# A block-sparse attention with a gated FFN on one Trainium2 core: the first pair's V on another queue, mask rows copied in pieces, the closing blocks in halves, and a new order of all instructions

## The chip, the cores and the metric

The kernel runs on one core of one Trainium2 chip. The metric is the device time of one execution in microseconds (us). Engines are named as in the profile: PE (TensorE matmuls), PEld (PE's weight loads, which overlap its matmuls), DVE (VectorE), ACT (ScalarE), POOL (GpSimd), SP (SyncE, which here only starts transfers). ACT, SP and POOL can each start DMA transfers.

## What is computed

The inputs are q, k and v (4 batches, 8 heads, 768 positions, 64 channels, float32), three sampled key blocks for each of 24 query blocks, and the weights of a gated convolutional feed-forward network.

```python
scores = (q @ k.T) / sqrt(64)
mask   = |blk_i - blk_j| <= 1  or first/last block row or column  or sampled
attn   = softmax(where(mask, scores, -1e9))
x      = (attn @ v), heads side by side          # (4, 768, 512)
h      = relu(x @ w_in)                          # (4, 768, 1024)
c      = conv of 3 taps along the sequence, per channel, with conv_w
out    = (h * sigmoid(c)) @ w_out                # (4, 768, 512) float32
```

## The kernel before, in words

**Tiling.** Two heads make a pair; there are 16 pairs P, four for each batch. The scores come transposed: 128 keys on the partitions, 128 queries in the columns. A pair has 6 key chunks and 6 query chunks for each head. The work of attention is cut into 144 units of eight 128x128 blocks: per unit two groups of score matmuls (line 761, "s"), one exponential of 128x1024 on ACT (line 773, "exp"), two groups of P-times-V matmuls (line 798, "av"). s writes one of two PSUM tiles st0 and st1, exp reads it and writes one of six SBUF tiles pt0 to pt5, and av accumulates in one of two PSUM banks, av0 and av1. V has a 65th column of ones, so the sums of the softmax come out of the same matmuls.

**The mask** needs no operation of its own: the operand tile T of a pair ("slot"; there are five) holds q and k transposed in rows 0 to 63 and, in rows 64 to 87, 24 rows that add -8000 to a masked block: columns 12 to 23 of T (chunks of 128) hold a one for a key's block, columns 0 to 11 the -8000 or 0 of the query's block. These rows are worked out once into slot 0 (line 276 "a1", 285 "a3", 306 "a4", 307 "a5", 314 "m_q0", 317 "m_q1", 322 "m_k", 349 "m_h1", 351 "m_r1"; `away` line 292) and copied to slots 1 to 4 (line 355, "m_slot", 24 partitions x 3072 on DVE). m_k copies from `nblk` (line 286), which is made from the identity matrix `ident`; POOL makes that (line 266) from a tile that DVE has set to zero (line 224), and POOL's DMA issues stand behind it in POOL's list.

**Loads.** The first pair's q, k and v come in float32 by the queues of SP and ACT (lines 244 to 262) and are cast on an engine: v by a copy of 128x768 ("v_cp", line 623). All other pairs come by POOL's queue, which casts to bfloat16 on the way; their V is copied into the tile with the column of ones on DVE or ACT (line 638). For P below 6, q and k are transposed on PE ("k_tr" line 469, "q_tr" lines 502 and 525) and copied from PSUM into the slot ("k_cp" line 480, "q_cp" lines 510 and 531); later ones use the DMA's transposing path (line 597). Units 0 to 17 are the first half of the queries of pairs 0 to 3; unit 4 is the first that needs pair 1, unit 9 pair 2, unit 13 pair 3. Units 18 to 35 are the second half.

**The FFN.** A batch's half of x is normalized (lines 707, 709), transposed, multiplied with w_in (line 895, "f1"), passed through relu by ACT or DVE (lines 915, 917), convolved on DVE (lines 953, 961), gated (lines 1000, 1003, 1008; "g2" is line 1008) and multiplied with w_out (line 830, "f2"), in blocks of 128 positions: `out_block` (line 816) accumulates 8 matmuls of 512 columns in one PSUM bank, copies 128x512 to SBUF ("ev", line 836) and writes it out (line 839). Only the very last block (positions 640 to 767 of the last batch) is done in two halves of 256 columns.

**What sets the order.** The program first makes a list of 1787 operations with their engines and buffers (class `Graph`, line 84). `put_down` (line 95) then walks the string `ORDER` (line 20): two characters give the number of an operation, a letter the engine where there is a choice (V is DVE, A is ACT), and further characters the buffers. So every engine's sequence, every choice between ACT and DVE and every buffer is written out by hand in this string. PE also runs 42 matmuls on zeros ("warm" of 256 columns and "fill" of 128, line 230) in the opening.

Of the kernel before, what the change touches and what calls it, by code (L numbers as in the profile page):

```python
# [25 lines left out]
2o34R1r2G04S2I01s1g4T2J4U6C16D6j26k6v1Z06l16z46L06M1l1p1+V6mV1/V6E51m1t4V2U14W1u4X2W24Y2X4Z1v4+6w6A6B6Q16R6F6N0
6G5U16S16V06W6X21w4/312506O06P6H06I6J05VV6T6+16/6KVih11k73074ii703ik01q2HV4ijV001o7547c17dil7e5in1ioipA17h07i
7m1imViF0iH7j0iGiIiq06U7n7o12b1ir2dV2cVisA7r06Y7s6Z7172767717A17B11iz1iA2Z07t27F07G7f7C32w0iBA2iJiN1iO7H4782iQ
797g7K12p12xV47L2rV2yV7k7l7p2qV7M57P07Q7qit02z17u7viP2BV2AV7w1iR7R07U17V7D0810iKiL7W12K12LV02MV7x82iuivV37E7I7J
7N8618733351347a17O7S7bV1832iS8838b07T7X7Z07Y18c7y08d4iT7+7zViM0iUiw1ixiyViV28g18h2Y1842N0858i58p08q8r0898a8u1  # L30
8v8e8f8j8k8w13522+361372OV2PViW8l28z08A8s08tiY8B27/18E18F8xiC08J08K8y80ViX8m8G38CiD8L48R18SiZ8T52VV0iEVj13j3j2
j918W08Xja8Y08n08D8H8/1908I9408M8oVi+8N1j42/V30Vj5911958U8V8Z8+jf096292jgi/j012j69c1j7j88O18P32V1939d9h09i97jh
jb9e49m19njijjV09j5jc9o139V38V523cjdA19r0989909a9s9w1jo0jp9t3jl11jjqA9x9E0jm9F3d13f9y09G2ju0jv3a0532C0542Q13e
9J19f09g3o3p03l3m1jwA9KjnVjJ0jK9k9O09P9l2D19pjL9L4jM2EV9Q5jr09q9ujs9vjN2FV3r3qjOjtVjR1jS3bV2jT9T19U9V1jA1jBjU
jx0jyjCAjzAjZ29/0a02R1a41a59z9B29A19H9I9M9N9R2TVa13a90aa9CjG08Q2j+jVk09ba602SAab2ae1afag4jD1jP9SjEjFVaj0akjH9W
jQj/jIVjk3h03t13i9D9Xa209Y19Za3k53k1al5jWa7a8acar1jXk6asaw0kj1axat3adahaiamaB1aCan1ay0auavazjYaD4k2kv0aG0aHk8
aI5k7k9ao0k3k4kaaO1kbkcaAkkaPaEaFkwaJaT0aKaL2aMaUkl3x3y23A3B2aQ1kxaY1aV29+3u3s4ap3g3aq03jV3kVkykzA2kmaZb103D3C
3Jb2knA3kB0kCkE1kFkDV14kGVkZ0k+a+3b303vVb61b7b84kN0kObe0aR1bfkQ1kRaSaWaXk/kPA5bj1bkkK0bg5kSAbl1l0l1l2kLbo0kW1a/
bpb0b4b5bt1b9buba0bq33M3N33K0aNbhld1kMVbv2kXbB0bCbikH0kYAbD03wVlf3nA3bG1kIbb1lelg3zV4bckT1bmbnbr3P3OkJV6bH3UbI4
3F03Q13Gl52l7kUkVV7l3bL0bMl6bN5kp0kqbsbwbxbQ1bRbS1bV0bWbdkokrkd1bE1bX33R3E0ll3lml8lol9lhlal41by0kAlblcbzlnlilp  # L40
ljc11ksbFbJbKbOc2c60c7c82ktA0bPbTbAkulk3IV3HVkekfkgc30cb0bUbYlt0lubZ0cccg1khA3lqlr3LV0b+2lscd4lvlz1chlAco0cplB
lCci5lwct1cuc4cq3lDA2lxA0cy0czc5lF13V23X3Y1403Zb/3+lGcv13SV13WV13TVlHVlI0lJcD1c9cElKVm10m2m3cacem4m5cA0cF2lO1cf
cI0cJcK4kilPlL0lMcjcklNAlQVm92ma410mbmcm6m7cl1cr1cQ1cRcS5cscwcV0cWcxcBcCcGcHlR0494a0c01ly4f1c+1c/cX13/46471cL
cN0mdd03lSd30d4lU1lVdb1dccOcmcncP42jelTAmelWVmh1mimjmfmkmgm84ed50dd2cM1cTcUcYcZlX0d1lYmllZVdg0dhdi4l+1l/dl1d2dm
d6d7dq0drm0Amp3de0d82dfdn54b4c4nds1mD1djdkdodpdv1dwdD0dEmx0mEmymmdx3mqd9msdtmrdudydz1dF2dI1dJmtmumnmo4o24s4ddG
dHdN0dOdK4mvmzmFdadP54kdS1dTdLmwmGdMd+0d/dQmA4pdA14l043V2mHV344VmBV0dU1e31dRe4e03dVdWdX0dBe52e80e9mV1mWea0mXV08
dYmY0mZe10e2m+Vnh0ninknjed1ee4glEn21e6m/0ei0ejn0n34B4C34qef4ek5n4A4Geq1ere7ebecegehelev04r4y4Des3n1V9np2nqnsnr
# [12 lines left out]
rn1qKrorC0rdr31rv0rwrDrpreArq1rrrEqTqMrx1rs0qZ0rtqNqOruryqVrzqPqQq+r4rR0rSrL1rMrNrOrTrUqWqXqYrPV1r5r6rVAr7A2q/  # L60
r0rWrQr8r1V0r2rF1rGrHrIrJA3rK
# [52 lines left out]
def kernel(  # L114
# [74 lines left out]
    op = gr.op  # L189
# [53 lines left out]
    vf = m_t[0].rearrange("p x y s -> p (x y s)")[:, 0:1536].bitcast(FP32)  # L243
# [4 lines left out]
    def first_k(x, e, prio, after):  # L248
# [11 lines left out]
    ld_v0 = dma("ld_v0", "SP", lambda: vf.rearrange("p (h c) -> p h c", h=2),  # L260
                v[0, 0:2].rearrange("h (p c) d -> p h (c d)", p=128), -18, service=1.6, after=[q1])
    ld_cw = dma("ld_cw", "SP", lambda: cw0, moe_conv_w.rearrange("k (f p) -> (k f) p", p=128), 8, service=0.05, after=[ld_v0])
# [85 lines left out]

    m_h1 = [op("m_h1", {"DVE": 0.25, "ACT": 0.37}, lambda e: dcopy(e, T_t[0][64:88, 6:11:2], T_t[0][64:88, 0:5:2]), T(0), m_q),
# [3 lines left out]
    mask_ready[(0, 1)] = m_h1  # L353
    for s in range(1, NSLOT):
# [48 lines left out]
    first_nq, first_q_sw = [], []  # L403
# [12 lines left out]
    def kq_transposes(P):  # L416
# [99 lines left out]
        def q_half(g, src, ldq, nbuf, pr):  # L516
            mb = Buf(P_mix)

            def fn(e):
                t = mix_t[mb.index].bitcast(BF16)  # L520
                for y in range(3):
                    nc.tensor.transpose(out=t[:, 128 * y:128 * y + 128], in_=src()[:, 128 * y:128 * y + 128], identity=ident)  # L522
            if P == 0:
                pr = T(14)
            tr = op("q_tr", {"PE": 0.168}, fn, pr, ldq + [o_ident], alloc=[mb], uses=[nbuf], after=k_trs[0:1])
            two = []
            for x in range(2):
                def cp(e, x=x):
                    dcopy(e, T_t[slot.index][0:64, 2 * x + g:2 * x + g + 9:4],
                          mix_t[mb.index].bitcast(BF16)[64 * x:64 * x + 64, 0:384].rearrange("p (c s) -> p c s", s=128))  # L530
                two.append(op("q_cp", {"DVE": t_d2(384) + 0.04, "ACT": t_act(384)}, cp, pr + 0.5 + 0.1 * x, [tr],
                              uses=[mb, slot]))
            for hh in range(2):
                qk_ready[(P, hh, g)] = (two + qk_ready[(P, hh, "k")] + mask_ready[(min(s, NSLOT - 1), hh)] +
                                        (m_r if P == 0 else []))
# [80 lines left out]
    def v_pair(P):  # L616
# [24 lines left out]
        in_turn("first" if P < NF else "v", lv)  # L641
# [21 lines left out]
    first_nq[0].after.append(first_q_sw[0])  # L663

# [151 lines left out]
    def out_block(b, t, due, deps, after, tail=False, last=False):  # L816
        gb, ob = gt_buf[b], Buf(P_os)
        halves = ((0, 256), (256, 512)) if last else ((0, 512),)
        outs = []
        for x, (c0, c1) in enumerate(halves):  # L820
# [6 lines left out]
            for a in range(4):  # L827
# [13 lines left out]
                due + 3, [evo], uses=[ob], dma=("hw", 0.65 if not last else 0.4)))  # L841
# [215 lines left out]
```

## Time and profile before

| | |
|---|---|
| median of 3 runs | 208.72 us (208.53 to 209.41) |
| span of the profiled execution, first to last instruction | 206.8 us |
| so around the span | 1.9 us |
| busy share PE, DVE, ACT, POOL | 96%, 90%, 92%, 30% |
| exp on ACT (144) | 140.6 us, 1048 ns each |

The span is the time between the first and the last instruction of one profiled execution. Busy time is a sum over stages; which engine sets the pace differs from stage to stage, and the ends of matmuls are modelled. A row of a timeline gives start, duration, engine, line, operation, output and input; a row of the chain of waits gives start, length and what held up the end there.

### The profile page before, as it was taken

How to read it: one execution, taken by the hardware profiler on the slowest of the kernel's cores; microseconds unless marked ns; L12 is line 12 of the kernel's file. 1: busy time of each engine (PE TensorE's matmuls, PEld its weight loads, DVE VectorE, ACT ScalarE, POOL GpSimd, SP SyncE). 2: the span in 40 equal slices, each digit the busy share in tenths (PEclk: the TensorE clock that was granted, in tenths of full speed). 3: DMA queues.
4: the chain of work that ended last, by engine and by line, in shares of the span. 5: the costliest groups of instructions: out<-in, count | busy, mean ns of one | idle time of the engine just before them, and what ended most of it. 6: DMA issues, size and time to landing. Idle time of an engine off the chain costs nothing.

```text
span 206.8 us, 6250 instructions
## 1 busy us (share of the span) xinstructions
PE 199.3 (96%) x2418; PEld 142.7 (69%) x2418; DVE 186.4 (90%) x576; ACT 190.6 (92%) x252; POOL 61.9 (30%) x113
## 2 busy tenths in 40 slices
PE   7799999999999999999999999999999999999992
PEld 5587878887567766766676767676667667786750
DVE  7999989999999998999789989999999938999970
ACT  6999999999999999999989998999999979997751
POOL 8696735302843233316054153800000000000000
PEclk9999999999999999999999999999999999999998
DMA  6999999998699976999969659999235131010414
GB/s 156 196 196 185 181 165 132 187 113 77 78 127 142 179 102 93 147 139 193 194 96 107 138 77 170 151 144 130 67 115 87 22 120 51 3 51 5 152 53 153
DMA packets 49305, 25.20 MB, mean 122 GB/s; under 512 B 35100, under 2 KB 46332, under 8 KB 49276
## 3 DMA queue, kind: packets, MB, share of 16 engines
q0 software_dynamic: 19728, 11.05, 44.9%
q1 hardware_dynamic: 29260, 13.46, 33.9%
q8 instruction: 19, 0.31, 0.6%
q10 hardware_dynamic: 288, 0.30, 0.4%
q14 instruction: 10, 0.08, 0.1%
HBM read 23.09 MB, written 6.29 MB: 142 GB/s over the span
## 4 chain that ended last, share of the span: by engine, by line
PE 71%; DVE 14%; ACT 11%; issue 2%; ACTq 0%
PE st L761 22%; PE mix L830 18%; PE mix L895 16%; PE av L798 12%; ACT pt L773 8%; DVE t L331 3%; DVE m L953 3%; DVE m L961 2%; DVE gT L1008 1%; ACT t L327 1%; DVE xtok L709 1%; PE st L830 1%; DVE hE L917 1%; PE mix L728 1%; DVE m L1003 1%
## 5 line engine op out<-in xcount | busy, mean ns | idle before, releaser
L773 ACT ACTIVATE pt<-st 128x1024 bf16<-128x1024 f32 x144 | 140.6, 1048 | 2.4 <-PE st L761 1.3
L761 PE MATMUL st<-t 88*128 88x256 bf16 (+2 forms) x600 | 90.0, 267 | 1.6 <-ACT t L327 0.8
L761 PEld LDWEIGHTS <-t 88*128 88x128 bf16 x600 | 48.5, 97 | 21.4 <-issue 1.6
L798 PEld LDWEIGHTS <-pt 128*128 128x128 bf16 x1152 | 52.2, 97 | 11.5 <-ACT pt L773 1.0
L798 PE MATMUL av<-vt,pt 128*128 128x65 bf16 x1152 | 58.4, 193 | 0.0
L895 PE MATMUL mix<-xT,winb 128*128 128x384 bf16 (+2 forms) x288 | 54.3, 308 | 0.3 <-ACT hE L915 0.2
L953 DVE TENSOR_SCALAR m<-hE,cw 128x382 bf16<-128x382 bf16 (+2 forms) x192 | 48.8, 316 | 0.4
L830 PE MATMUL mix<-woutb,gT 128*128 128x512 bf16 x184 | 48.7, 379 | 0.2 <-DVE gT L1008 0.2
L961 DVE TENSOR_TENSOR m<-m 128x764 bf16<-128x764 bf16 (+2 forms) x64 | 33.8, 534 | 0.6
L895 PEld LDWEIGHTS <-winb 128*128 128x128 bf16 x288 | 24.4, 97 | 9.4 <-issue 0.8
L1000 ACT ACTIVATE m<-m 128x764 bf16<-128x764 bf16 (+2 forms) x32 | 26.8, 840 | 1.1 <-DVE m L961 1.0
L407 POOL COPY pace<-pt 1x1 bf16<-1x1 bf16 x24 | 9.6, 402 | 53.3 <-ACT pt L773 53.3
L830 PEld LDWEIGHTS <-gT 128*128 128x128 bf16 x200 | 17.3, 97 | 11.7 <-DVE gT L1008 1.1
L915 ACT ACTIVATE hE<-mix 128x384 bf16<-128x384 f32 (+2 forms) x36 | 17.7, 507 | 1.7 <-PE mix L895 1.6
L917 DVE TENSOR_SCALAR hE<-mix 128x384 bf16<-128x384 f32 x28 | 15.5, 557 | 4.1 <-PE mix L895 3.7
L1008 DVE TENSOR_TENSOR gT<-m,hE 128x764 bf16<-128x764 bf16 (+3 forms) x36 | 18.2, 511 | 0.6
L709 DVE TENSOR_TENSOR xtok<-av,rcp 128x384 bf16<-128x384 f32 (+2 forms) x36 | 18.1, 508 | 0.5
L239 POOL DMA_DIRECT2D nat<-in_q_dram x23 | 17.0, 738 | 2.1 <-issue 1.4
L331 DVE COPY t<-mix 64x384 bf16<-64x384 bf16 (+1 forms) x33 | 13.4, 413 | 0.7 <-PE mix L522 0.2
L327 ACT COPY o2s<-mix 128x512 f32<-128x512 f32 x17 | 9.9, 598 | 2.9 <-PE mix L830 2.7
L1003 DVE TENSOR_SCALAR m<-m 128x764 bf16<-128x764 bf16 (+3 forms) x36 | 12.1, 335 | 0.5 <-ACT m L1000 0.4
L239 POOL DMA_DIRECT2D vn<-in_v_dram x15 | 11.3, 756 | 1.9 <-DVE vt L331 1.4
(75 smaller groups left out, 118.4 us busy)
## 6 DMA issues: line engine op xcount, KB each, us to landing
out_dram<-o2s SPq DMA_DIRECT2D x23, 256.0 KB, 2.9
nat<-in_k_dram POOLq DMA_DIRECT2D x15, 192.0 KB, 4.2
vn<-in_v_dram POOLq DMA_DIRECT2D x15, 192.0 KB, 5.7
nat<-in_q_dram POOLq DMA_DIRECT2D x6, 192.0 KB, 4.9
winb<-in_moe_w_in_dram POOLq DMA_DIRECT2D x2, 512.0 KB, 7.3
woutb<-in_moe_w_out_dram POOLq DMA_DIRECT2D x4, 256.0 KB, 6.7
nat<-in_q_dram POOLq DMA_DIRECT2D x9, 96.0 KB, 5.2
nq<-in_q_dram POOLq DMA_DIRECT2D x6, 96.0 KB, 5.1
```

What stands on the lines that cost most here:

```text
L239: return op(name, {eng: occ}, lambda e: on(e).dma_start(out=dst(), in_=src), prio, deps, dma=(kind, service), **kw)
L331: nc.vector.tensor_copy(out=dst, in_=src)
L709: nm = op("norm", {"DVE": t_dps(128 * C)}, lambda e: nc.vector.tensor_tensor(out=xtok_t[xk.index][:, 0:C].rearrange("p c h d -> p h c d"), ...
L761: nc.tensor.matmul(out=st[:, 128 * x:128 * (x + n_)], lhsT=t[0:88, 12 + 6 * hh + kc, :], rhs=t[0:88, idx:idx + (n_ - 1) * (2 if P < NPE el ...
L773: nc.scalar.activation(out=pt_t[ptb.index][:, c0:c1], in_=st_t[stb.index][:, c0:c1], func=AF.Exp, bias=0.0, scale=0.125)
L798: nc.tensor.matmul(out=o[:, off:off + 65], lhsT=pt_t[ptb.index][:, 128 * x:128 * x + 128], rhs=V_t[vslot_b[P].index][:, hh, kc, 0:65], sta ...
L830: nc.tensor.matmul(out=acc(), lhsT=gT_t[gb.index][:, ffc, 128 * t:128 * t + 128], rhs=woutb[:, ffc, c0:c1], start=(ffc == 0), stop=(ffc == ...
L895: nc.tensor.matmul(out=mix_t[hb.index][:, w1 * y:w1 * y + w1], lhsT=winb[:, fc, 128 * ffc:128 * ffc + 128], rhs=xT_t[xt_buf[n].index][:, f ...
L953: nc.vector.tensor_scalar(out=m_t[cb.index][:, x, y, 0:w], in0=hE_t[heb.index][:, f0 + y, t0 + x:t0 + x + w], scalar1=cw[:, x, f0 + y:f0 + ...
L961: nc.vector.tensor_tensor(out=m[:, a_, :, 0:w], in0=m[:, a_, :, 0:w], in1=m[:, b_, :, 0:w], op=ALU.add)
L1000: th = [op("tanh", {"ACT": t_act(2 * w) + 0.04}, lambda e, cb=cb, w=w: nc.scalar.activation(out=m_t[cb.index][:, 0, :, 0:w], in_=m_t[cb.in ...
L1008: nc.vector.tensor_tensor(out=gT_t[gtb.index][:, f0:f0 + 2, t0:t1], in0=m_t[cb.index][:, 0, :, 0:w], in1=hE_t[heb.index][:, f0:f0 + 2, 1 + ...
```

## The change

It has four parts.

1. **V of pair 0.** `ld_v0` (float32 by SP's queue into a spare tile) and its cast are gone; pair 0 gets V like the others, in bfloat16 by POOL's queue, with the transfer behind pair 1's q. The copy into the tile with ones, which ACT did, is now given to DVE.
2. **Mask rows.** Slot 1's copy of 24x3072 becomes three: the key columns (24x1536, m_sk), the query columns of the first half (24x768, m_sq) and, later, of the second half (24x768, m_sr). Slot 4's copy becomes a transfer by SP (m_sp). Slots 2 and 3 stay.
3. **Closing blocks.** The two blocks before the last one (positions 384 to 639 of the last batch) are also done in two halves of 256 columns each.
4. **`ORDER`** is another string, for 1801 operations.

```diff
-    ld_v0 = dma("ld_v0", "SP", lambda: vf.rearrange("p (h c) -> p h c", h=2),
-                v[0, 0:2].rearrange("h (p c) d -> p h (c d)", p=128), -18, service=1.6, after=[q1])
...
+    def rows_to(s, c0, c1, step):
+        return lambda e: dcopy(e, T_t[s][64:88, c0:c1:step], T_t[0][64:88, c0:c1:step])
...
     for s in range(1, NSLOT):
-        mr = [op("m_slot", {"DVE": 0.95}, lambda e, s=s: dcopy(e, T_t[s][64:88], T_t[0][64:88]),
-                 T(4.5 * s - 2.5), m_h1 + m_r, earliest=7.0 + 2 * s)]
+        mask_g1[s] = []
+        if s == 1:
+            mr = [op("m_sk", {"DVE": 0.53}, rows_to(1, 12, 24, 1), T(2), m_k + m_h1[1:]),
+                  op("m_sq", {"DVE": 0.33}, rows_to(1, 0, 11, 2), T(2), m_q + m_h1[:1])]
+            mask_g1[s] = [op("m_sr", {"DVE": 0.33}, rows_to(1, 1, 12, 2), T(12), m_r)]
+        elif s < NSLOT - 1:
+            mr = [op("m_slot", {"DVE": 0.95}, lambda e, s=s: dcopy(e, T_t[s][64:88], T_t[0][64:88]),
+                     T(4.5 * s - 2.5), m_h1 + m_r, earliest=7.0 + 2 * s)]
+        else:
+            mr = [dma("m_sp", "SP", lambda s=s: T_t[s][64:88].rearrange("j c s -> j (c s)"),
+                      T_t[0][64:88].rearrange("j c s -> j (c s)"), T(4.5 * s - 2.5), m_h1 + m_r, service=0.3)]
...
-        if P == 0:
-            def cp(e):
-                dcopy(e, V_t[vs.index][:, :, :, 0:64], vf.rearrange("p (h c d) -> p h c d", h=2, c=6))
-            v_ready[P] = op("v_cp", {"DVE": 0.5, "ACT": t_act(768)}, cp, due + 1, [ld_v0] + v_one, alloc=[vs], earliest=8.5)
-            in_turn("vs", v_ready[P])
-            return
...
-        halves = ((0, 256), (256, 512)) if last else ((0, 512),)
+        halves = ((0, 256), (256, 512)) if last or (b == B - 1 and t > 2) else ((0, 512),)
```

The string itself says nothing to a reader. Decoded, the lists of the engines begin like this (numbers count the operations of a name; for copies of q and k, cp means from PSUM).

```
ACT before: q0, k0 issues; m_k0; cast q0, k0, k0; m_q0 twice; q_cp (pair 0); m_q1; m_h1; exp 0; exp 1; v_cp (pair 0); exp 2 ...
ACT after:  q0, k0 issues; m_k0; cast q0, k0, k0; k_cp, q_cp, k_cp (pair 0); cast q0; k_cp (pair 0); exp 0; exp 1; exp 2 ...

DVE before: ones, zeros of hE; zeros of warm, of ident; a1; a3; nblk; m_k1; ident24; m_h1; ones; a4; a5; a5; k_cp; ones, ones;
            k_cp; k_cp; ones; k_cp; m_r1; cast q0; m_slot 1; q_cp (all pair 0); k_cp, k_cp, q_cp, q_cp (pair 1); m_slot 2; cw; diag 4;
            q_cp, q_cp (pair 0, second half); v_cp (pair 1); k_cp, q_cp, q_cp, k_cp (pair 2); rcp, norm 0; v_cp (pair 2);
            m_slot 3; k_cp, k_cp, q_cp, q_cp (pair 3); m_slot 4; rcp, norm 1 ...
DVE after:  a1; a3; ones (3); zeros of warm, of ident; nblk; ident24; ones; m_k1; a4; zeros of hE; a5; ones; m_h1; m_q0 twice;
            k_cp (pair 0); a5; m_sk; m_h1; q_cp (pair 0); m_sq; k_cp, k_cp, q_cp, q_cp (pair 1); m_q1; v_cp (pair 0); m_r1; cw;
            q_cp, q_cp (pair 0, second half); m_slot 2; k_cp, k_cp, q_cp, q_cp (pair 2); v_cp (pair 1); m_slot 3; rcp; v_cp (pair 2);
            norm 0; k_cp, k_cp, q_cp, q_cp (pair 3); diag 4, 6; q_cp, q_cp (pair 2, second half); m_sr; rcp, norm 1 ...

POOL before: iota; ident; loads k1, q1, q0 second half, v1, k2, q2, q1 second half, v2, q2 second half, k3, q3, v3, k4 ...
POOL after:  iota; ident; loads k1, q1, v0, q0 second half, v1, k2, q2, v2, k3, q1 second half, q3, q2 second half, v3, k4 ...
```

In both, pair 0's first av stands behind s of some units on PE: before behind those of units 2 and 3, after behind those of units 4 and 5. Later the two strings hold the same units in the same order, with the FFN's parts at places that differ by a few groups of matmuls. Of the relus of batch 0's first half, two that ACT did (the third and the seventh) are DVE's now; of its second half the first went from DVE to ACT. At the end, PE's last matmuls were those of positions 512 to 639 (8 of 512 columns); now they are the second half of positions 384 to 511 (8 of 256 columns), behind 16 of 256 columns for positions 512 to 639.

More of the change, by code (lines that the diff above doesn't have):

```diff
@@ L26 @@
[L26 to L35, printed above, removed]
@@ new lines @@
+ef0egmZA0846Vn0Ve4n11e8eh04f4m4u4r4n14s4D4E34tek1ele9n2edeeem54I4A4F4B24G4Hnj0nkn3V9nld+nmes0etein70ejn41eneu3ex1n5
+n6Aeyeo1evn8ez1eC0eDna1mEdE24ilA4v0ep1eqernr1n9VansnbnnncV4jV34kVnz2eE44OeH1eIng0nheweAeBeFeP0eJ0eGnd1eKniAno4P0eQ
+eR2eLnemL0eU1eVnueM0nAeNnfAbnH3ntnpnvnInCnBeZ0e+mMmNeW54l47d/mK4weO4J14KlGe/3f21f3nK4oV3nDnJ4CV4nq0f41mR1eS0nwnx
+4xV4nynLf70f8mOmPA1eTff1mSmTeXfgf90nEeYmUmVA0f0fk0f1flf5fh4fm2f6fao50o81o9o6fc1oaVfp1o7Afqfb1fin/1fu0fr5nMnF4yVnG
+ov0ownNo20o0o3o1Vo4Aon1fdnOfjfnfofvfsfC1ftfDnV0fw3fE1oyopoxoznWfH0fIfJ0nXnYnZA3fM1fxfNfO4fyob1fR0fSfF0fGoe0oc4LV0
@@ L62 @@
+hE0hP0hhVhz1pCApShAVpYp/3hQhY1hZhFhJqs0qm1qnq0hR3hL0q1hMq2pZq3h+1i10hK1hSi2hTqoAgqtq71ia1ibq8h/0hU1p+qD0q4q5hVq6
+quAhqT1qUqVqWqEi30hN0q9qai0hOA2ic4qj0qki4qbA1i51idieqp1qlAii62i7i80if0qv2qwqxigqGqqi9Aqd0qrAjqehW1qfhXVih1qgiiArq1
+rrqFqyqHqzqhA0rh0rirsAqArjAqL3qNqXqBqCrn1rorpAqIrt0rk0rup8qcpeqirv2qMqJrwqKqOrxqPrlrmArD1q/1rEry0rzqYrA0rF2qQrBqZrG
+rCrHqRr0rZ0rI0s31r50rJr6rK0qSr+r/s4s5r7r1rLrMq+r8r2s0s6r9V3r3A1s1A2rarN0rOrT1rPrQs7ArRA0r4s8s2rSrUrVrWrb0rcrXArYrd
+rerfArg
 """
@@ L259 @@
     ld_q0, ld_k0 = [q0, q1], [k0, k1]
-    ld_v0 = dma("ld_v0", "SP", lambda: vf.rearrange("p (h c) -> p h c", h=2),
-                v[0, 0:2].rearrange("h (p c) d -> p h (c d)", p=128), -18, service=1.6, after=[q1])
-    ld_cw = dma("ld_cw", "SP", lambda: cw0, moe_conv_w.rearrange("k (f p) -> (k f) p", p=128), 8, service=0.05, after=[ld_v0])
+    ld_cw = dma("ld_cw", "SP", lambda: cw0, moe_conv_w.rearrange("k (f p) -> (k f) p", p=128), 8, service=0.05, after=[q1])
     o_iota = op("iota", {"POOL": 0.15}, lambda e: nc.gpsimd.iota(apart_i, pattern=[[1, NB]], base=64,
@@ L402 @@
     k_first, slot_first, fine = {}, {}, {}
-    first_nq, first_q_sw = [], []
+    first_nq, first_q_sw, first_v = [], [], []
     def pace(u, prio):
@@ L534, in q_half @@
                 qk_ready[(P, hh, g)] = (two + qk_ready[(P, hh, "k")] + mask_ready[(min(s, NSLOT - 1), hh)] +
-                                        (m_r if P == 0 else []))
+                                        (mask_g1[min(s, NSLOT - 1)] if g else []))
         if P == 0:
@@ L640, in v_pair @@
                         [lv] + v_one, alloc=[vs], uses=[vb], earliest=9.0 + 2 * P if P < NF else 0.0)
-        in_turn("first" if P < NF else "v", lv)
+        if P == 0:
+            first_v.append(lv)
+        else:
+            in_turn("first" if P < NF else "v", lv)
         if b == 1:
@@ L663 @@
     first_nq[0].after.append(first_q_sw[0])
+    first_v[0].after.append(first_q_sw[0])
     seq = [SWQ[(x[:-1], int(x[-1]))] for x in
@@ L840, in out_block @@
                 out=out[b, 128 * t:128 * t + 128, c0:c1], in_=o2s_t[ob.index][:, c0:c1]),
-                due + 3, [evo], uses=[ob], dma=("hw", 0.65 if not last else 0.4)))
+                due + 3, [evo], uses=[ob], dma=("hw", 0.65 if len(halves) == 1 else 0.4)))
     def whole_gate(n, heb, gtb, base, W):
```

63 lines of the change are left out of this document (31 added, 32 removed).

## The prediction

> **What bounds the kernel now.** I read the page first, then the busy time by stage, then the chain of waits in order of time.
>
> ```profile
> span 206.8 us, 6250 instructions
> PE 71%; DVE 14%; ACT 11%; issue 2%; ACTq 0%
> ```
>
> The first row is the time to account for: 206.8, with 1.9 around it up to the median of 208.72. The second says that the end is held by PE for 71% of the span; where DVE and ACT hold it, the stages tell.
>
> ```profile
> 0.00:7.60 7.60, 5.66 (x48) 4.42 (x49) 6.10 (x29) 5.20 (x10) 6.42 (x14) 1.00 0.77 169
> 7.60:20.60 13.00, 12.43 (x181) 9.76 (x180) 12.42 (x30) 12.94 (x14) 9.30 (x16) 1.00 1.35 191
> ...
> 30.00:56.00 26.00, 25.89 (x370) 19.71 (x367) 25.50 (x74) 26.00 (x32) 11.20 (x21) 1.00 1.06 116
> 56.00:190.00 134.00, 133.51 (x1584) 93.73 (x1585) 123.34 (x370) 129.15 (x170) 29.94 (x52) 1.00 0.73 111
> ```
>
> Behind the length stand the busy times of PE, PEld, DVE, ACT and POOL. From 56 to 190 PE is busy 133.51 of 134.00: whatever order its work has, this stage can give about 0.5 and no more by this view. In the opening ACT is the full one (12.94 of 13.00). From 30 to 56 ACT, PE and DVE are all full (26.00, 25.89, 25.50). So a gain has to come from the opening, where ACT gets its first exponential late, or from the last 17 us.
>
> ```profile
> 2.37 0.56 DVE nblk L286
> ...
> 5.54 0.60 ACT t L327 x2
> 6.17 0.47 ACT t L327
> ...
> 7.61 1.94 ACT pt L773 x2
> 9.57 0.83 ACT vt L327
> 10.40 0.93 ACT pt L773
> ...
> 19.54 1.89 ACT pt L773 x2
> 21.55 1.03 ACT pt L773
> ...
> 55.55 0.57 DVE gT L1008
> 56.16 1.04 PE mix L830 x4
> ...
> 199.44 3.50 PE mix L830 x16
> 202.95 0.59 ACT o2s L327
> ```
>
> These pieces of the chain are start, length and what held the end. ACT copies mask rows and q up to 7.61, runs two exps, stops them for V's cast (9.57, 0.83), and goes on. At 19.54 one piece holds two exps in 1.89 and the next exp starts only at 21.55, so the second one began late, at about 20.6. At 55.55 DVE hands over to PE. At the end PE runs 16 matmuls, ACT copies 0.59, and 3.2 us of transfer and closing follow 203.54.
>
> **The change part by part. The opening.** The lists in the section on the change say what each engine does first; I put the durations of before on them.
>
> ```profile
> 1.07 0.11 DVE L224 MEMSET ident<- 128x64 uint32 x1
> 1.22 0.17 DVE L271 CAST apart<-apart_i 24x24 f32<-24x24 int32 x1
> 1.26 0.29 POOL L266 TENSOR_SCALAR_AFFINE_SELECT ident<-ident 128x128 bf16<-128x128 bf16 x1 [0.28 <-DVE ident L224]
> 1.50 0.83 POOL L239 DMA_DIRECT2D nat<-in_k_dram  x1
> 2.16 0.17 DVE L282 SCALAR_TENSOR_TENSOR A<-keyid,A 24x24 f32<-24x24 f32 x1
> 9.16 0.34 PEld L460 LDWEIGHTS <-nat 128*128 128x128 bf16 x6 [0.27 <-DMA nat<-in_k_dram]
> ```
>
> POOL's select waited for DVE's zeros, and its first issue stands behind that select. In the new list a1 and a3 (1.22 to 2.33, so 1.1 us) and three short memsets stand ahead of the zeros. If a1 starts at about 1.05, when the iota is there, the zeros end at about 2.5, the select runs 2.6 to 2.9, nblk starts at 2.95 in place of 2.37 (+0.6), and POOL's first issue at 2.85 in place of 1.50 (+1.35). Behind that issue stand all loads of POOL, V0 now among them. Does anybody wait? Before, pair 1's k landed at 9.16, with the V of 384 KB on the other queue beside it. I take 6.5 to 7.5 after the change (an estimate: 7.7 passed between the issue at 1.50 and the first use at 9.16; without V on the other queue I let about half of that stand, 3.7 to 4.7 behind 2.85). Its transposes are wanted at about 8.6, so the delay is hidden; uncovered it costs up to 1.35.
>
> ACT's own list: m_k starts with nblk's end, 3.5. Then come the casts, three k copies and a q copy, with exp 0 behind. The first two rows below are of before, the others are groups.
>
> ```profile
> 2.96 0.70 ACT L327 COPY t<-nblk 24x384 bf16<-24x384 bf16 x1
> 3.69 1.23 ACT L327 CAST nat<-o2s 128x192 bf16<-128x192 f32 x3
> ...
> L331 DVE COPY t<-mix 64x384 bf16<-64x384 bf16 x23 | 8.1, 353 | 0.6 <-PE mix L522 0.2
> L331 DVE COPY t<-nblk 24x384 bf16<-24x384 bf16 x1 | 0.5, 484 | 0.0
> L331 DVE COPY t<-t 24x384 bf16<-24x384 bf16 x1 | 0.3, 283 | 0.0
> L331 DVE COPY vt<-vn 128x768 bf16<-128x768 bf16 x14 | 5.1, 361 | 0.0
> L331 DVE CAST nat<-o2s 128x192 bf16<-128x192 f32 x1 | 0.3, 260 | 0.0
> L379 DVE TENSOR_SCALAR diag<-ident,cw 128x128 bf16<-128x128 bf16 x24 | 4.5, 267 | 0.0
> L917 DVE TENSOR_SCALAR hE<-mix 128x384 bf16<-128x384 f32 x28 | 15.5, 557 | 4.1 <-PE mix L895 3.7
> L915 ACT ACTIVATE hE<-mix 128x384 bf16<-128x384 f32 x28 | 13.8, 510 | 1.4 <-PE mix L895 1.3
> ```
>
> m_k takes 0.70, three casts 1.23, a fourth about 0.3 and four copies 0.47 each (as the q copy at 6.17): 4.1 from 3.5, so exp 0 starts at about 7.7, 0.1 later than 7.61. Exps 0 and 1 take 1.94; exp 2 then starts at 9.6 and not at 10.4, because V's cast is DVE's: 0.7 earlier. Exp 4 is the first that needs pair 1. Its four copies take 1.88 on DVE (as pair 3's in the next fence) and start at about 9.2, an estimate from DVE's list with nblk at 2.95, no longer behind k's landing; they end at 11.1, and with half a us for scores exp 4 starts at 11.6. So far ACT leads by about 0.5.
>
> Then DVE has to keep up. Up to pair 3's last q copy, which ended at 20.10,
>
> ```profile
> 18.22 1.88 DVE L331 COPY t<-mix 64x768 bf16<-64x768 bf16 x4
> 20.13 0.95 DVE L331 COPY t<-t 24x3072 bf16<-24x3072 bf16 x1
> ```
>
> DVE loses three k copies (3 x 0.35), a cast (0.26), a whole-slot copy (0.95) and one diagonal (three of 24, 4.5 / 8 = 0.56): 2.8. It gains m_q0 in two pieces and m_q1, m_h1, m_sk, m_sq and V's copy. The strided mask copies of 24x384 lie between 0.28 and 0.48 in the rows above; I take 0.45 for each of m_q0 and m_q1, nearest to the nblk copy, because they too gather; m_h1 is 0.28; m_sk, half of 24x3072, between 0.48 and 0.95, I take 0.53; m_sq 0.38, between the rows of 384 and 3072 by size; V's copy 0.36. Sum 2.45 (2.1 to 3.0). So the list is 0.4 shorter, but nblk is 0.6 later: the copies end at about 20.3, exp 13 starts 0.2 late. ACT's lead of 0.5 ends there. Behind it ACT no longer does the third relu (0.51) ahead of exp 24, so at about 31 the exps lead by 0.3 (between +0.8 if DVE keeps up and -0.6 if the strided copies take the upper ends).
>
> **30 to 56.** ACT loses another relu (0.51). DVE gets both (2 x 0.56), loses the first relu of the second half (0.56) and slot 4's copy (0.95, now SP's transfer, which nobody waits for until unit 36, some 30 us later) and gains m_sr (0.38). With the 0.4 from above DVE is 0.4 lighter up to there, but it starts 0.6 late. I count nothing for this stage and carry the 0.3; if DVE's idle time (0.5 in this stage) does not take it up, it costs 0.2 to 1.7.
>
> **56 to 190.** The same matmuls by another order: nothing, between -0.5 (PE's idle time) and +1.
>
> **The end.** Two blocks more in halves add no columns: 16 of 256 for 8 of 512, twice. The last eviction gets half as wide:
>
> ```profile
> 199.22 0.43 DVE L1008 TENSOR_TENSOR gT<-m,hE 128x512 bf16<-128x512 bf16 x1
> ...
> L327 ACT COPY o2s<-st 128x256 f32<-128x256 f32 x1 | 0.4, 372 | 0.7 <-PE st L830 0.7
> ...
> out_dram<-o2s SPq DMA_DIRECT2D x6, 256.0 KB, 2.5
> ```
>
> 0.37 for 0.59 gives 0.2, and the last transfer is half as large; the landing of a half is not shown, it saves between 0 and 1.25 (half of 2.5). I take 0.2, nearer to nothing, since 2.5 for 256 KB is mostly not payload at the rates of the stages. But DVE's last g2, which ended at about 199.65, has more of PE's work behind it: 3.7 for 3.0 us by columns. If DVE and not PE sets the time there, 0.7 is lost. I take a gain of 0.3, between +0.4 and -0.3.
>
> Sum: 0.3 + 0 + 0 + 0.3 = 0.6. 206.8 becomes 206.2, and with 1.9 around it the time is 208.1.
>
> **The rivals. Relief of ACT counts in full** (faster). ACT's list is shorter by m_q0, m_q1, m_h1, V's cast and two relus, 3.4 in all, and longer by three k copies and a cast, 1.7. If the strided copies cost 0.28, exps keep a lead of 0.8 to unit 36, PE gets fed earlier by that, the end gives 0.4, and PE's 0.5 idle time goes: 208.7 - 1.7 = 207.0 (206.3 to 207.6). For it: ACT is the full engine in every stage to 56. Against: exp 13 waited for DVE already before, at 20.6.
>
> **DVE becomes the bound before 56** (slower). It starts 0.6 late and takes two relus, 1.1, and at 55.55 it is DVE that releases PE. If slot 4's copy filled a pause before, its removal gives nothing, and g2 at 55.55 comes 0.6 + 1.1 = 1.7 later, less 0.3 at the end: 208.7 + 1.4 = 210.1 (209.7 to 210.6). It decides once DVE's list to g2 is longer by more than its idle time of about 0.5. For it: 25.50 of 26.00 busy, and DVE's 14% of the chain. Against: its list got no longer in sum.
>
> **PE's slow opening lasts longer.**
>
> ```profile
> 1.15:3.90 2.75, 2.73 (x13) 1.94 (x14) 1.00 0.73 208
> ```
>
> The 13 matmuls of 256 columns on zeros took 2.73, 0.21 each, although the granted clock says 1.00; in the end stage 16 of 512 took 3.50, 0.22 for twice the columns. So PE began at half rate. Its first matmul waits for DVE's zeros, at about 2.5 in place of 1.17, and a pause for the casts follows. If the half rate lasts through unit 0, two groups of scores of 512 columns and six transposes cost 0.5 to 0.8 more; pair 1's wait at 11.1 swallows 0.4 of it. That gives 208.4 (208.2 to 209.0). [...]
>
> **The change does not do what it says:** POOL's list is late by 1.35 and V and k come no earlier than before, so exps 4 and on keep their places. With 0.3 from the end: 208.4 to 208.8.
>
> **How the numbers follow.** A measurement of this kernel can tell about 0.5%, 1.04 us, from no change: 207.7 to 209.8. Forecast 208.1 (207.7 to 208.7): 0.34. Relief in full: 0.34. DVE the bound: 0.22. Slow opening 0.06 and no effect 0.04, both within 0.5%. Faster 0.34, same 0.44, slower 0.22. The range, 206.4 to 210.2, leaves out the ends of both outer cases, about 0.1 and 0.08.
>
> **What would show it.** Right: exp 0 at 7.6 to 8.0, exp 2 within 2.0 of it, exp 13 at 20.4 to 21.0, pair 1's k landed before 8, the first f2 at 55.5 to 56.5, the last eviction 0.37, PE still over 99% busy from 56 to 190. Wrong: exp 4 later than 12.1 (DVE's list is slower than summed), pauses of PE for DVE between 30 and 56 of more than 0.5, or PE idle by over 1 us after 56, which no part of this sum foresees.

## The result, and the profile after

The changed kernel takes 210.93 us (median of 4 runs, 210.58 to 211.57) against 208.80 for the kernel before in the same runs (208.53 to 209.41): a ratio of 1.0104, with a 95% interval of 1.0088 to 1.0120. It is 2.1 us slower, and that lies outside the predicted range.

The page's first row and the shares of the chain of waits, after:

```profile
span 209.7 us, 6265 instructions
PE 65%; DVE 21%; ACT 10%; issue 2%; POOL 0%; POOLq 0%; ACTq 0%
```

The profiled execution took 211.57, the slowest of the four, so its times below lie up to 0.6 above those of a middle one; again 1.9 lie around its span. DVE's share of the chain went from 14 to 21%. Busy time by stage, cut at the events that cut the stages before (exponential 0 and exponential 13, now at 9.10 and 23.47), with one row for a stretch near the end. The columns are the stretch, its length, then busy time and count of PE, PEld, DVE, ACT and POOL, then granted clock, DMA share and GB/s:

```profile
0.00:9.10 9.10, 6.09 (x36) 4.27 (x37) 6.65 (x30) 5.29 (x11) 6.78 (x15) 1.00 0.81 138
9.10:23.47 14.37, 13.22 (x188) 10.59 (x187) 11.98 (x30) 12.30 (x13) 10.84 (x18) 1.00 1.17 165
33.00:59.00 26.00, 25.51 (x372) 19.70 (x373) 25.63 (x78) 25.45 (x30) 10.35 (x22) 1.00 1.02 129
59.00:186.00 127.00, 126.18 (x1485) 88.37 (x1497) 117.39 (x347) 122.81 (x159) 30.23 (x52) 1.00 0.72 115
186.00:189.20 3.20, 3.02 (x43) 2.36 (x42) 3.20 (x11) 2.15 (x4) 0.00 (x0) 1.00 0.03 8
```

The opening up to exponential 0 is 1.5 longer and the next stage 1.4 longer, and in both ACT now has more than it needs (12.30 of 14.37, where it was full before). On balance nothing more is lost up to 130: the exponentials (counted from 0) stand 2.85 later at number 13, 2.83 at 48 and 2.33 at 130. Then it grows to 3.70 at number 143. Not all of that growth is a loss: run 5 below, without the stall described here, also goes from 0.13 early at 130 to 0.86 late at 138, and is 0.05 early at 143. The two places are the opening and the last row.

**The opening.** PE's own instructions in order of time (start, length, line, output and inputs, shape of one, count), after, and then two rows of before:

```profile
2.57 2.10 PE L229 MATMUL av<-warm 128*128 128x256 bf16 x9 [2.57 <-DVE warm L222]
5.11 0.50 PE L469 MATMUL mix<-ident,nat 128*128 128x128 bf16 x3 [0.44 <-ACT nat L323]
...
8.43 1.49 PE L768 MATMUL st<-t 88*128 88x256 bf16 x6
...
10.92 0.73 PE L469 MATMUL mix<-ident,nat 128*128 128x128 bf16 x6
11.49 0.60 PE L768 MATMUL st<-t 88*128 88x256 bf16 x4
```

```profile
1.17 3.68 PE L230 MATMUL av<-warm 128*128 128x256 bf16 x23 [1.17 <-DVE warm L223]
...
9.16 0.51 PE L460 MATMUL mix<-ident,nat 128*128 128x128 bf16 x6
```

The same six transposes take 0.73 after and 0.51 before: 0.107 from start to start against 0.055. PE goes at half rate from its first matmul at 2.57 up to about 11.4; before it was from 1.17 to 4.35. This spacing is what is called half rate below. No column of the profile says so: the granted clock is 1.00 in both. The first pieces of DVE and POOL came as the prediction had them; behind them the chain is PE's:

```profile
2.22 0.17 DVE vt L368 x3
2.66 0.30 POOL ident L262
2.99 0.56 DVE nblk L282
...
8.63 1.28 PE st L768 x6
10.02 0.46 PE av L509 x3
10.48 0.65 PE av L229 x5
11.13 0.53 PE mix L469 x6
```

Where ACT's exponentials stood in the chain of before, there is now PE, and DVE behind it: it waited 1.8 for the transposes of the second half's q at 10.

**Near the end.** ACT, DVE and PE by time, after (in brackets the idle time ahead and who ended it):

```profile
188.66 0.55 DVE L1015 TENSOR_TENSOR gT<-m,hE 128x764 bf16<-128x764 bf16 x1
189.96 0.68 DVE L960 TENSOR_SCALAR m<-hE,cw 128x256 bf16<-128x256 bf16 x3 [0.75 <-ACT hE L922]
...
189.32 0.60 ACT L922 ACTIVATE hE<-mix 128x512 bf16<-128x512 f32 x1 [1.17 <-DVE gT L1015]
...
189.98 0.22 PE L735 MATMUL mix<-ident,xtok 128*128 128x128 bf16 x1 [0.90 <-ACT hE L922]
```

A relu of ACT (number 59 counted from 0, for positions 384 to 639 of the last batch) waits 1.17 for a g2 of DVE (number 27, for positions 0 to 381 of that batch); PE waits 0.90 and DVE 0.75 for that relu. Nothing of the kind stood in the chain before. At the very end the last eviction is 0.37, as forecast:

```profile
206.40 0.37 ACT o2s L323
```

### The profile page after: what moved, and what is told of

Same layout as the page of the kernel before. It is cut to its first block, busy times and chain, and to the rows that moved or that the text cites. A ratio compares the mean times of both kernels' runs of the same rounds, so it can differ in the third digit from the quotient of the medians.

```text
span 209.7 us, 6265 instructions
## 1 busy us (share of the span) xinstructions
PE 199.6 (95%) x2415; PEld 145.0 (69%) x2434; DVE 186.1 (89%) x581; ACT 189.8 (91%) x250; POOL 61.7 (29%) x114
## 4 chain that ended last, share of the span: by engine, by line
PE 65%; DVE 21%; ACT 10%; issue 2%; POOL 0%; POOLq 0%; ACTq 0%
PE st L768 20%; PE mix L837 16%; PE mix L902 12%; PE av L805 11%; ACT pt L780 7%; DVE t L327 5%; DVE m L960 4%; DVE m L968 2%; DVE hE L924 2%; ACT hE L922 2%; DVE xtok L716 2%; PE av L229 1%; DVE gT L1015 1%; PE st L837 1%; PE av L979 1%
## 5 line engine op out<-in xcount | busy, mean ns | idle before, releaser
L768 PE MATMUL st<-t 88*128 88x256 bf16 (+2 forms) x600 | 92.5, 270 | 1.7 <-DVE t L327 1.1
L805 PEld LDWEIGHTS <-pt 128*128 128x128 bf16 x1152 | 55.7, 97 | 14.7 <-ACT pt L780 0.3
L805 PE MATMUL av<-vt,pt 128*128 128x65 bf16 x1152 | 62.7, 193 | 0.1
L960 DVE TENSOR_SCALAR m<-hE,cw 128x382 bf16<-128x382 bf16 (+2 forms) x192 | 50.2, 318 | 1.8 <-ACT hE L922 1.5
L837 PE MATMUL mix<-woutb,gT 128*128 128x512 bf16 (+1 forms) x181 | 46.3, 360 | 0.6
L837 PEld LDWEIGHTS <-gT 128*128 128x128 bf16 x216 | 18.4, 97 | 11.1 <-DVE gT L1015 3.3
L416 POOL COPY pace<-pt 1x1 bf16<-1x1 bf16 x24 | 8.5, 353 | 51.8 <-ACT pt L780 51.6
L924 DVE TENSOR_SCALAR hE<-mix 128x384 bf16<-128x384 f32 x30 | 16.7, 555 | 5.0 <-PE mix L902 4.8
L922 ACT ACTIVATE hE<-mix 128x384 bf16<-128x384 f32 (+2 forms) x34 | 16.7, 507 | 2.0 <-DVE gT L1015 1.2
L323 ACT COPY o2s<-mix 128x512 f32<-128x512 f32 (+1 forms) x18 | 10.1, 561 | 4.2 <-PE mix L837 3.7
```

What stands on the lines that cost most here:

```text
L768: nc.tensor.matmul(out=st[:, 128 * x:128 * (x + n_)], lhsT=t[0:88, 12 + 6 * hh + kc, :], rhs=t[0:88, idx:idx + (n_ - 1) * (2 if P < NPE el ...
L805: nc.tensor.matmul(out=o[:, off:off + 65], lhsT=pt_t[ptb.index][:, 128 * x:128 * x + 128], rhs=V_t[vslot_b[P].index][:, hh, kc, 0:65], sta ...
L837: nc.tensor.matmul(out=acc(), lhsT=gT_t[gb.index][:, ffc, 128 * t:128 * t + 128], rhs=woutb[:, ffc, c0:c1], start=(ffc == 0), stop=(ffc == ...
L922: nc.scalar.activation(out=dst, in_=src, func=AF.Relu, bias=0.0, scale=0.5)
L960: nc.vector.tensor_scalar(out=m_t[cb.index][:, x, y, 0:w], in0=hE_t[heb.index][:, f0 + y, t0 + x:t0 + x + w], scalar1=cw[:, x, f0 + y:f0 + ...
```

## The experiments

All times are medians of the runs that they are compared in; the kernel before was run beside each and stood at 208.63 to 208.69.

**1 to 4: PE's clock.** Theory: the half rate is the cost of the opening. In the decoded lists (- is the old place, + the new one):

```diff
  DVE (1 and 4):
+ zeros of warm, of ident
  a1; a3; ones (3)
- zeros of warm, of ident
  nblk ...
  PE (1):
- warm (9); k_tr ...
+ warm (13), fill (10); k_tr ...
  PE (2, zeros as in the changed kernel):
- warm (9); k_tr ...
+ warm (11); k_tr ...
  kernel before (3):
- prev = op("warm" if x < NWARM else "fill", {"PE": 0.213 if x < NWARM else 0.107}, warm_mm, -20
+ prev = op("warm" if x < NWARM else "fill", {"PE": 0.213 if x < NWARM else 0.107}, warm_mm if x >= 23 else None, -20
```

> The kernel after the change, with DVE's zeros of warm and of ident back at the head of DVE's list and all 13 warm and the first 10 fill matmuls back ahead of the first k transpose, as before; nothing else. Theory clock (PE starts 1.4 late and with pauses, so it runs at half rate to 11.4 and the opening loses 1.5 at exp 0 and 2.85 at exp 13): full rate by about 4.4, exp 0 at 7.3 to 7.9, exp 13 at 20.2 to 20.9, time 207.6 to 209.0. Rival DVE (its longer list of mask copies is the cause): exp 0 early, but exp 13 still at 22 or later and the time over 210. Rival order (the loss arises after 30 us): exp 13 early and the time still over 210.

> The kernel after the change with two warm matmuls of 256 columns moved ahead of the first k transpose, so that PE has no pause at 4.7 to 5.1; the zeros stay late. [...] If only the late start counts, or DVE: no change, 210.6 to 211.2.

> The kernel before the change, without the 13 warm and first 10 fill matmuls (matmuls on zeros that no result uses); all lists else as before. Theory clock: PE stays at half rate to 7.8 or 11.2, exp 13 comes 1 to 3 later than 20.6 and the time is 209.7 to 211.7. Rivals DVE and order: the time stays at 208.5 to 209.2, since DVE's list and the later order are untouched.

> The kernel after the change with only DVE's zeros of warm and of ident at the head of its list; PE's order stays, so PE runs 9 warm matmuls from 1.1 to 3.0 and then pauses for the first k transpose until about 4.5. If a pause of 1.5 us keeps the clock low: half rate to about 7.8 or later, exp 0 at 8.0 to 8.8, time 209.0 to 210.4. If only the start of PE counts: as e1_clock_early within 0.4. Rival DVE: over 210.4, as POOL's loads were not the wait.

Measured: 208.88 (1; 208.63 to 210.14, 10 runs), 210.11 (2; 209.55 to 210.32), 210.13 (3; 209.54 to 210.37), 210.90 (4; 210.65 to 211.12; four runs each), against 210.93 for the changed kernel and 208.66 for before. PE's rows of each, in that order:

```profile
1.06 4.02 PE L229 MATMUL av<-warm 128*128 128x256 bf16 x23 [1.06 <-DVE warm L222]
...
8.04 0.50 PE L469 MATMUL mix<-ident,nat 128*128 128x128 bf16 x6
```

```profile
2.57 2.53 PE L229 MATMUL av<-warm 128*128 128x256 bf16 x11 [2.57 <-DVE warm L222]
...
9.71 0.50 PE L469 MATMUL mix<-ident,nat 128*128 128x128 bf16 x6
```

```profile
4.48 0.50 PE L460 MATMUL mix<-ident,nat 128*128 128x128 bf16 x3 [4.48 <-ACT nat L327]
...
10.20 0.85 PE L460 MATMUL mix<-ident,nat 128*128 128x128 bf16 x6
```

```profile
1.06 2.10 PE L229 MATMUL av<-warm 128*128 128x256 bf16 x9 [1.06 <-DVE warm L222]
4.64 0.50 PE L469 MATMUL mix<-ident,nat 128*128 128x128 bf16 x3 [1.48 <-ACT nat L323]
...
10.23 0.50 PE L469 MATMUL mix<-ident,nat 128*128 128x128 bf16 x6
```

By the spacing of the matmuls, half rate ends at about 5.8, 8.6, 12.0 and 9.9. With zeros first and no pause ahead of the transposes (1), 2.05 of the loss are gone. Run 4 has DVE's and POOL's lists of run 1, with POOL's first load at 1.44 as there (2.90 in the changed kernel), and differs from it only in the place of the zero matmuls: PE stands still for 1.48, and the median is that of the changed kernel. So neither an early first matmul nor early loads win anything by themselves; the zero matmuls that keep PE busy up to the first transposes give the 2.0. Run 3 takes the same thing from the other side: the kernel before loses 1.5 when PE has no work ahead of its first transpose. In its profile the exponentials stand 1.62 late at number 2, between 1.60 and 1.77 from there on and 1.66 at the end: no later stage takes up what the opening lost. In run 2 two more of the zero matmuls ahead of the transposes, 0.43 of PE's time that computes nothing, win 0.8.

The order alone does not fix where the half rate ends. Run 10, further below, has the changed kernel's opening word for word. Up to 8.43 its PE rows start within 0.01 of those of the changed kernel, and there the same six matmuls take 0.87 and not 1.49:

```profile
8.43 0.87 PE L768 MATMUL st<-t 88*128 88x256 bf16 x6
...
9.86 0.50 PE L469 MATMUL mix<-ident,nat 128*128 128x128 bf16 x6
```

Its half rate ended at 8.5, that of the changed kernel at 11.4, and its exponential 13 came 1.67 late and not 2.85. One profile of an order therefore shows one such end, not the order's own. The profiles with PE's opening of before (before, 6, 7 and both builds of 8) have it between 4.2 and 6.1, those with the opening of run 1 (1, 5, 9, 11) between 4.5 and 6.9, the other five between 8.5 and 12.0. These groups do not overlap, so that zeros first and no pause end it earlier is shown. That closing the pause alone does so, as run 2 was to tell, is not: its 8.6 is no earlier than run 10's 8.5, and only its median speaks for it.

**5, 7 and 10: which of the two waits.** In `ORDER` of before, that relu's word stands ahead of the g2; in the changed one right behind it. They touch the same two rows of hE at different columns (the g2 reads 1 to 382, the relu writes 385 to 640), and the one that stands later in the string is made to wait. No engine's own list changes in these runs:

```diff
  5 (on run 1) and 10 (on the changed kernel):
  tanh 27 (ACT)
+ relu 59 (ACT)
  g1 27; norm 33; g2 27 (DVE)
- relu 59 (ACT)
  7 (on the kernel before):
- relu 59 (ACT)
  g2 26; rcp 33; g1 27; g2 27 (DVE)
+ relu 59 (ACT)
```

> The order with the clock mended, and one word of the order string moved: the relu of the last half that writes rows 6 and 7 beyond column 384 now stands ahead of the g2 that reads the columns below it, as it does in the order before. No engine's own list changes, only which of the two waits for the other. Theory 1 (the stall of PE near 186 to 189 comes from that direction of the wait): the relu no longer waits 1.2 for g2, the pause of PE of about 1.06 goes, and the time falls from 208.9 to about 207.8, below both kernels. Rival (DVE's list is late there by its own work, and g2 only happens to be the last of it): the relu starts earlier but the exponential behind it gains nothing or PE waits for another of DVE's results; less than 0.3 gained, 208.6 to 208.9.

> The mirror of the first run: the kernel before, with the same relu's word moved behind that g2 in the order string. No engine's list changes. Theory 1 (direction of the wait): ACT waits for g2 at about 186, the exponential behind the relu and x's transposes come late, and the time grows by 0.8 to 1.2, to 209.5 to 209.9. Rival (DVE's list): nothing, 208.5 to 208.9.

> The changed kernel as it is, PE's late clock with it, and only the relu's word moved ahead of that g2. If the two losses add up, it gains the same 1.0 as with the clock mended: 209.8 to 210.0. Rival (behind the late clock the end meets other waits, so that the stall is partly hidden): 210.2 to 210.9.

Measured: 207.84 (5; ratio to before 0.9960, 0.9948 to 0.9973), 209.83 (7; 1.0061, 1.0048 to 1.0073) and 209.66 (10; 1.0054, 1.0037 to 1.0071). The rows by time of run 5, then of run 7:

```profile
185.59 0.59 ACT L922 ACTIVATE hE<-mix 128x512 bf16<-128x512 f32 x1
...
186.22 0.56 DVE L1015 TENSOR_TENSOR gT<-m,hE 128x764 bf16<-128x764 bf16 x1
...
186.45 0.22 PE L735 MATMUL mix<-ident,xtok 128*128 128x128 bf16 x1
```

```profile
187.34 0.60 ACT L913 ACTIVATE hE<-mix 128x512 bf16<-128x512 f32 x1 [1.10 <-DVE gT L1006]
...
187.99 0.22 PE L726 MATMUL mix<-ident,xtok 128*128 128x128 bf16 x1 [1.02 <-ACT hE L913]
```

In run 5 the relu runs ahead of the g2 and nobody waits; in run 7 the stall stands in the kernel before, with 1.10 and 1.02. The word's place is worth 1.04 one way, 1.15 the other and 1.27 in the changed kernel as it is, the last from 4 and 6 executions that spread over 1.0 and 1.4. Run 5 is faster than both kernels. Why two pieces without a common element are ordered at all, no run here shows.

**6: the closing halves alone**, in the kernel before, on the block that ends its program; in `ORDER` DVE then evicts the first half and ACT, as before, the second:

```diff
-        halves = ((0, 256), (256, 512)) if last else ((0, 512),)
+        halves = ((0, 256), (256, 512)) if last or (b == B - 1 and t == 4) else ((0, 512),)
```

> The kernel before with its very last block (16 matmuls' worth of columns that end the program) in two halves of 256 columns, evicted and sent one by one; nothing else changes. Theory 1 (the end is set by the last eviction and the last landing, as the runs with the new closing order suggest, which gained 0.55 to 0.66 behind PE's end): 0.35 to 0.65 faster, 208.1 to 208.4. Rival of the prediction's sum (0.2 of the eviction, and a landing that hardly depends on size): 0.2 faster, 208.5. No gain at all if the first half's transfer holds up the second.

Measured: 208.20 (208.07 to 208.45, 11 runs), ratio 0.9978 (0.9969 to 0.9987): 0.48 faster. PE ends as before (0.04 earlier); the last eviction starts at the same time and takes 0.37 for 0.59:

```profile
202.91 0.37 ACT o2s L325
```

So 0.22 is the eviction, and by the medians the other 0.26 lies behind it, with the transfer of half the size: from the end of the last eviction to the end of the span it is 2.94 here and 3.24 before. In all profiles with halves it is 2.84 to 2.94, in all with a whole block 3.24 to 3.31.

**8: V by POOL alone**, in the kernel before:

```diff
-    ld_v0 (SP, float32, behind q0)            v_cp of pair 0 (ACT, between exp 1 and exp 2)
+    ld_v of pair 0 (POOL, behind q1's load)   v_cp of pair 0 (DVE, behind pair 1's q copies)
```

> The kernel before with the first part of the change alone: the first pair's V comes by GpSimd's queue in bf16 behind the second pair's first q, and DVE copies it behind the second pair's q copies; ACT's cast of it goes. PE's opening clock is as before. Theory 1 (DVE's list up to pair 3's copies sets exponential 13, ACT's relief is used up there): exponential 2 about 0.7 earlier, exponential 13 within 0.4 of before or later by DVE's copy (0.36), the end within 0.4: 208.4 to 209.1. Rival (relief of ACT counts in full, as one of the prediction's rivals has it): exponentials lead by 0.7 from 13 on and the time falls by 0.5 to 0.8, 207.9 to 208.2.

> Mends the run before of this edit, in which the fourth pair's V was loaded into the first pair's buffer ahead of the copy, so that the first pair got the fourth's V and PE stood still until it landed at 16.3. Now that load waits for the copy. The kernel before with the first part of the change alone: the first pair's V by GpSimd's queue in bf16, copied by DVE behind the second pair's q copies. Theory 1 (DVE's list up to pair 3's copies sets exponential 13, ACT's relief is used up there): exponential 2 about 0.7 earlier, exponential 13 within 0.4 of before or later by DVE's copy (0.36), the end within 0.4: 208.4 to 209.1. Rival (relief of ACT counts in full): exponentials lead by 0.7 from 13 on, 207.9 to 208.2.

The first build took 217.02. It loads the fourth pair's V into the first pair's buffer ahead of the copy, so its time says nothing of this part. The second took 209.75 (ratio 1.0052, 1.0040 to 1.0064): 1.06 slower, more than either theory had. DVE and ACT by time:

```profile
8.55 0.95 DVE L326 COPY t<-t 24x3072 bf16<-24x3072 bf16 x1
9.53 0.35 DVE L326 COPY t<-av 64x384 bf16<-64x384 bf16 x1
9.81 1.87 DVE L326 COPY t<-mix 64x768 bf16<-64x768 bf16 x4
11.71 0.36 DVE L326 COPY vt<-vn 128x768 bf16<-128x768 bf16 x1
...
10.46 2.85 ACT L766 ACTIVATE pt<-st 128x1024 bf16<-128x1024 f32 x3 [0.92 <-PE st L754]
```

ACT is rid of V's cast and gains nothing: it waits 0.92, because exponential 2 needs q's second half, and its copy on DVE (9.53) stands behind the whole-slot mask copy. DVE gets 0.36 more, and exponential 13 is 0.49 late. So in the kernel before this part does not pay. That it pays together with the mask pieces, which take that copy out of the way, is a reading of runs 1 and 5, in which exponential 2 is 0.9 early and which hold the other parts too; the mask pieces alone were not tried.

**9 and 11: what DVE's list is worth**, both on run 5:

```diff
  9:
- k_cp (pair 2, first): DVE
+ k_cp (pair 2, first): ACT
  11:
- m_sp (SP's transfer of slot 4's mask rows)
+ m_slot 4 (DVE, 0.95, behind pair 3's copies)
```

> The mended kernel of 207.84 with one letter of the order changed: the first of pair 2's k copies is ACT's and not DVE's (0.57 off DVE, 0.47 onto ACT, where ACT waited 0.5 for that pair). Theory 1 (DVE's list up to pair 3's copies is what holds the exponentials, and what is won there stays to the end as the rigid shift of the run without the first zero matmuls suggests): exponential 13 earlier by 0.3 to 0.6 and the time 207.3 to 207.6. Rival (between 30 and 56 ACT and DVE are full and take it back, or ACT's own copy delays the exponentials by its 0.47): exponential 13 no earlier, or earlier and the end unmoved, 207.7 to 208.3.

> The mended kernel of 207.84 with the fifth slot's mask rows copied by DVE again (0.95, in the place that they had before: behind the copies of pair 3) and not by a transfer of SP. It prices one term of the prediction, which took that copy's removal from DVE for about nothing. Theory (the term as priced: the 0.95 falls on idle time of DVE or PE behind exponential 13): exponential 24 and on within 0.3, the time 207.7 to 208.1. Rival (DVE is full from 20 to 56, so its list stands 0.95 later at unit 30 and PE waits for it): 0.4 to 0.95 slower, 208.2 to 208.8.

Run 9 took 207.88 and tells the theories apart only in part. What it was to give never came: the pair's second k copy, still DVE's, waited for ACT's, and DVE lost 1.0 instead of winning 0.57. From the waits:

```profile
DVE t L327 <- ACT t L323: 1.0, 1, 1.0
```

Exponential 13 came 0.13 later and the end did not move.

Run 11 took 209.15 (208.61 to 209.92, 12 runs) against 207.84: 1.3 slower, beyond the rival's 0.95. In its profile (208.61, its fastest run) DVE's next copies, for pair 2's second half, start at 22.61 and not at 21.43:

```profile
20.23 1.28 DVE L327 COPY t<-t 24x3072 bf16<-24x3072 bf16 x1
21.53 1.07 DVE L388 TENSOR_SCALAR diag<-ident,cw 128x128 bf16<-128x128 bf16 x6
22.61 0.72 DVE L327 COPY t<-mix 64x384 bf16<-64x384 bf16 x2
```

The copy itself took 1.28 here, and not 0.95. Exponential 13 is 0.23 earlier than in run 5, which the edit does not explain: the half rate ended at 4.5 in this profile and at 6.9 in that of run 5, and exponential 0 already stands 0.50 earlier. Exponential 18 is 1.06 later; 0.68 of it is left at the end. The other 0.5 between that execution and the median is not explained.

## Why the prediction was wrong, point by point

- **The step that failed is "PE's slow opening lasts longer"**, which was no part of the sum but a rival with a chance of 0.06 and 0.3 us. The half rate was named and its price was wrong by a factor of seven: 2.05 (run 1 against the changed kernel). It let the half rate last "through unit 0" and priced a few instructions of that unit. In the changed kernel's profile it lasted to 11.4 (8.5 in that of run 10), through unit 1's scores (in the row at 8.43) and into pair 1's transposes (10.92) too, and delayed exponential 0 by 1.49 and the copies that DVE has to make from the transposes. "Pair 1's wait at 11.1 swallows 0.4 of it" fell as well: pair 1's copies began at 11.7 and not at 9.2, because the q transposes that DVE waited 1.8 for stood in the same slow queue.
- **How long the half rate lasts: measured, and not explained.** From the first matmul to full rate it took 3.2 before, 4.7 (run 1), 6.0 (2), 7.5 (3), and 8.8 where PE paused (1.48 in run 4, 0.44 after), but 5.9 in run 10 with the same pause as after. What ends it, and so what a pause costs beyond these cases, no run here shows. Nor does a run show what the expected ends rest on, 7.8 or 11.2 in run 3 and 7.8 or later in run 4; it ended at 12.0 and at 9.9.
- **nblk, POOL and the loads: right.** nblk at 2.99 (2.95), POOL's first issue at 2.90 (2.85), pair 1's k landed at 6.5 (6.5 to 7.5), m_k at 3.57 (3.5).
- **The lists of ACT and DVE: near in run 5, in part by luck.** Run 5 shows exponential 0 at 7.58 (7.7), exponential 2 at 9.40 (9.6), exponential 4 at 11.51 (11.6), pair 3's copies done at 20.43 (20.3) and exponential 13 0.33 late (0.2). But its zeros stand first, so nblk starts at 2.52, 0.4 earlier than the sum had it. By that sum the copies should then have ended at about 19.9; they ended at 20.43, and at 20.20 in run 11, so DVE's list up to there took 0.3 to 0.5 more than was added up. By ACT's list (4.1 behind m_k, which makes 7.6 from 3.5, and m_k starts at 3.11 here) exponential 0 should have come near 7.2; it does so in run 11 (7.08), where the half rate ended at 4.5. In the changed kernel itself exponential 0 came at 9.10 and 13 2.85 late.
- **A lead of 0.3 at 31: wrong by half a us**, in run 5 still 0.22 late at exponential 24.
- **Slot 4's copy: counted with 0.95 in a balance that came to nothing; worth 0.8 by the profile of run 11 and 1.3 by its median.** So the size fits. That this is what pays for DVE's two relus, and why the rival "DVE becomes the bound" did not come about in run 5, is a reading; the relus were not moved back.
- **56 to 190: "nothing, between -0.5 and +1" was right as a bound and wrong as a value.** The order brought one stall of 1.04, at the upper end; the prediction's own test ("PE idle by over 1 us after 56, which no part of this sum foresees") is what happened. No engine's own list shows it.
- **The end: 0.3 forecast, 0.48 measured** (run 6). The eviction's 0.22 was right; the half transfer gives 0.26 by the medians, and 0.3 to 0.4 in the profiles, where I took 0.2, with 0.1 off again for a loss at DVE's last g2 that did not show. The reason given, that 2.5 for 256 KB is "mostly not payload at the rates of the stages", does not come out of the rows: at their 111 to 191 GB/s, 256 KB alone take 1.4 to 2.4.

The account, from medians: 208.68 for before beside run 5; 2.05 for the clock, 1.04 for the relu's place, and -0.84 for all the rest of the change (run 5 against before; the halves alone gave -0.48 in run 6), together the measured 210.93. These are differences of the same medians, so they add up by construction; what backs them from outside are runs 7 and 10 for the relu, and 3 and 4 for the clock. The forecast for that rest was -0.6, 0.3 before the end and 0.3 there. The profile of run 5 has PE end 0.23 earlier than before and the other 0.61 behind it. So what was changed on purpose did about what was forecast in sum, and two things that came along with the new order cost 3.1.

## What to carry to other kernels

Price a late or interrupted start of PE by the time to its full rate (3.2 to 8.8 in these profiles) and not by the instructions of the first unit: read the start-to-start times of equal matmuls (0.107 and 0.055 here), since the granted clock said 1.00 in the openings of both kernels, and read them in more than one execution, since one order gave 8.5 and 11.4. When an order is searched anew, compare more than the engines' lists: for pairs of operations on one tile, see which of them stands later in the string, because here that one waited (1.17 in the changed kernel, 1.10 in run 7) although the two share no element. Zero matmuls that left a pause of 1.48 ahead of the first real one won nothing (run 4); without the pause they won 2.0 (run 1).

## What the runs showed of the hardware

- The half rate at the start isn't in the granted clock: 1.00 in the openings before and after, whether equal matmuls started 0.107 apart or 0.055. In the first build of run 8 the granted clock did fall: PE stood still from 12.2 to 16.75, and the page's row shows 0.5 in the slice from 16.2 to 21.6 (40 slices of 5.4 us, in tenths):

```profile
PEclk9985799999999999999999999999999999999999
```

- A loss of 1.62 at the exponential near 12 us came out as 1.66 at the last one (run 3), through 177 us in which ACT and DVE have idle time of their own (129.15 and 123.34 busy of 134.00 from 56 to 190, before). Behind 30 us PE is over 99% busy in the stages shown of the kernel before (25.89 of 26.00, 133.51 of 134.00), and the shift passed through whole.
- With one and the same opening the half rate ended at 8.5 and at 11.4 (run 10 and the changed kernel), at 4.5 and at 6.9 (runs 11 and 5).
- The spread of a kernel's runs differs between orders: run 5 stayed within 0.03 us (5 runs), run 10, the same order with the late clock, within 1.41 (6 runs), and run 11, with the early clock, within 1.31 (12 runs). Executions with different ends of the half rate may be part of it, but only one execution of each order has a profile, so why is open.
